# A decode attention kernel whose big loads move from SyncE's DMA queue to GpSimd's

## The chip, the core and the metric

The kernel runs on one core of a Trainium2 chip. A core has five engines with an instruction stream each: TensorE (PE; PEld is its weight load), VectorE (DVE), ScalarE (ACT), GpSimd (POOL) and SyncE (SP). They meet only through semaphores. Data comes from HBM into SBUF, an on-chip memory of 128 partitions, by DMA: an engine issues a transfer, 16 DMA engines carry it out, and a semaphore tells that it has landed. TensorE writes its results to PSUM, a second on-chip memory. The metric is the device time of one execution in microseconds; less is better.

## The reference

Eight sequences, one new token each, 32 heads of 128, and a cache of 4096 keys and values per head. All inputs are bf16.

```python
xn = layernorm(x)                                  # (8, 1, 640)
q = (xn @ wq) as (8, 32 heads, 1, 128)
p = softmax(q . k_cache / sqrt(128))               # k_cache, v_cache (8, 32, 4096, 128)
attn = (p . v_cache) joined over heads @ wo        # wo (4096, 640)
y = layernorm(xn)
mlp = gelu(y @ w1 + b1) @ w2 + b2                  # w1 (640, 1728), w2 (1728, 640)
out = x + attn + mlp
```

The two caches are 8 x 32 x 4096 x 128 x 2 bytes = 268.4 MB each. They are read once. With the weights this is nearly all that the kernel moves.

## The kernel before

The work is cut into 32 tiles (`NQ = 32`), each of 8 heads of one sequence. A tile of K, and a tile of V, is one load of 128 partitions x 64 KB = 8.39 MB: a partition holds 256 consecutive keys of one head. SBUF has three slots of this size in the tensor `S_sb`: K tiles alternate between slots KA and KB, all V tiles use the slot VS. The same slots hold the weights where no tile needs them: `wq` lies in VS at the start, the MLP weights in KA and the output weights `wo` in KB at the end.

What happens to a tile i:

- K(i) lands. POOL has waited for it and writes a flag, the memset of `kr_sb` (`k_ready`), which releases TensorE; VectorE waits for K(i) itself.
- For 80 of a partition's 256 keys, TensorE transposes K in groups of eight (`pe_T`, into `TR_ps`), ScalarE copies them to `KT_sb` (`act_T`), and TensorE multiplies with the query (`pe_QK`, into `S_ps`). The last of them gives the ticket `kt` or `qkl`.
- For the other 176 keys VectorE does it in three chunks (`dve_chunk`): multiply by the query in place (ticket `ym`), add one half to the other, reduce (the last chunk's ticket is `km`).
- VectorE finds the maximum (`dve_max`), ScalarE does the exponentials into `P_sb` (`act_exp`, ticket `exp`).
- When V(i) has landed, TensorE multiplies it with `P_sb` (`pe_PV`, 256 matmuls into `PV_ps`, ticket `pv`), ScalarE copies the result to `oU_sb`, and POOL scales it into `oT_sb` (`o_norm`).
- POOL also spreads the next tile's query over partitions (`qrep`, the copy to `qrep_sb`), once the last `pe_QK` of the tile before is done.

The order on each engine is written out by hand: `at(position, function, ...)` puts a step at a position on one axis, 100 per tile (`Q = 100.0`), and the steps are then called in that order, each adding its instructions to the lists of the engines it uses. An engine takes its own list strictly in order, and a wait holds all that stands behind it on that engine.

All big loads are on SyncE's list, K(i+1) ahead of V(i). K(i) waits until its slot is free: for i from 2 to 5 for `kt` and `km` of tile i-2, from `KLATE = 6` on for `exp` of tile i-2. V(i) waits for `pv` of tile i-1; V(0) and K(1) wait for `qmm`, the end of the query's matmuls. V(30), the last but one, is loaded in two pieces (`V_CUT`, 192 and 64 keys of each partition), so that `pe_PV` of tile 30 can start on the first; for this TensorE's loop has one more wait at key 192, on the semaphores `ld_vl`. The MLP weights (`load_mlp`) are issued after V(30), the output weights in six pieces (`load_wl`, `load_wn`) after V(31), which waits for `pv` of tile 30. Eight small loads (`load_w2b`) follow POOL's memset of their place. At the end the pieces of `wo` are multiplied in as they land, and the output is stored.

The profile knows nearly every instruction as line 111, the helper that writes it out (109 for waits); the tensor's names tell the steps apart.

Of the kernel before, what the change touches and what calls it, by code (L numbers as in the profile page):

```python
# [14 lines left out]
P = 128  # L15
# [177 lines left out]
def bass_parallel_sum__gqa_block_cached__mixer_channel_mlp__decode_kernel(  # L193
# [21 lines left out]
    NQ = NHQ * B  # L215
    DC = D // P
    FB = F // P
# [11 lines left out]
    NS = 2  # L229
    LOOP0, LOOPN = 2, 15  # L230
    KLATE = 6
    assert NKEY == 256 and NQ == 32
    SLOT = NKEY * DH
    KA, KB, VS = 0, 1, 2
# [1 line left out]
    RW = P // HW  # L236
    NL = 3
    WN_CUT = (0, 5 * CT, 7 * CT, 7 * CT + CT // 2, HS * CT)
    V_CUT = (0, 192, 256)

    def jp_of(i):
        return 80

    def chunks(i):
        jd = NKEY - jp_of(i)
        n = 3
        return [(jd * c // n, jd * (c + 1) // n) for c in range(n)]

    def kslot(i):
        return KA if i % 2 == 0 else KB  # L250
# [8 lines left out]
    with ExitStack() as es:  # L259
        sb = lambda name, shape, dt: es.enter_context(nc.sbuf_tensor(name, shape, dt))  # L260
        ps = lambda name, shape, dt: es.enter_context(nc.psum_tensor(name, shape, dt))
        sem = lambda name: es.enter_context(nc.semaphore(name))

        S_sb = sb("S_sb", [P, 3, SLOT], BF)
        tile = [S_sb[:, s, :].rearrange("p (j d) -> p j d", d=DH) for s in range(3)]
# [6 lines left out]
        def scratch(n, rows=P, slot=KB):  # L272
            ap = part(slot, o_[slot], n, rows)
            o_[slot] += n + n % 2
            return ap

        wq_sb = part(VS, 0, DC * H * DH).rearrange("p (c n) -> p c n", c=DC)
        w1_sb = scratch(DC * F, P, KA).rearrange("p (c n) -> p c n", c=DC)
        w2_sb = scratch(FB * D, P, KA).rearrange("p (c n) -> p c n", n=D)
# [20 lines left out]
        zeros_sb = scratch(P)  # L300
        assert max(o_.values()) <= SLOT

        ones_sb = sb("ones_sb", [1, B], BF)
# [16 lines left out]
        mx_sb = sb("mx_sb", [P, 32], F32)  # L320
        mxT_sb = sb("mxT_sb", [P, 32], F32)
        mq_sb = sb("mq_sb", [P, 2], F32)
        mb_sb = sb("mb_sb", [P, 32], F32)
# [20 lines left out]
        pe, dve, act, sp, pool = (_Eng(sem(f"{n}_s")) for n in ("pe", "dve", "act", "sp", "pool"))  # L344
        pe2, act2, fin, fin2 = (_Eng(sem(n)) for n in ("pe2_s", "act2_s", "fin_s", "fin2_s"))
        ld_s = [_Dma(sem(f"ld_s{s}")) for s in range(3)]
        ld_x, ld_b1, ld_b2, ld_wq, ld_w1, ld_w2a, ld_w2b, st_a, st_o = (
            _Dma(sem(n)) for n in ("ld_x", "ld_b1", "ld_b2", "ld_wq", "ld_w1", "ld_w2a", "ld_w2b", "st_a", "st_o"))
        ld_vl = [_Dma(sem(f"ld_vl{q}")) for q in range(1, len(V_CUT) - 1)]
        ld_wl = [_Dma(sem(f"ld_wl{q}")) for q in range(2)]  # L350
        ld_wn = [_Dma(sem(f"ld_wn{q}")) for q in range(len(WN_CUT) - 1)]
        tk = {}
        prog = []

        def at(pos, fn, *a):
            prog.append((pos, len(prog), fn, a))

        def load(key, dma, dst, src, eng=None):
            tk[key] = dma.sig((eng or sp).dma_start(dst, src))

        def cache_src(cache, i):
            hq, b = divmod(i, B)
            return cache[b, hq * HS:(hq + 1) * HS].rearrange("h (p j) d -> (h p) j d", j=NKEY)

        def load_k(i):
            s = kslot(i)
            if i >= KLATE:
                sp.wait(tk[("exp", i - 2)])
            elif i >= 2:
                sp.wait(tk[("kt", i - 2)], tk[("km", i - 2)])  # L370
            elif s == KB:
                sp.wait(tk["qmm"])
            tk[("k", i)] = ld_s[s].sig(sp.dma_start(tile[s], cache_src(A_k_cache, i)))

        def load_mlp():
            sp.wait(tk[("kt", NQ - 2)], tk[("km", NQ - 2)])
            load("w1", ld_w1, w1_sb, B_w1.rearrange("(p c) f -> p c f", c=DC))
            load("w2a", ld_w2a, w2_sb, B_w2[0:FB * P, :].rearrange("(p c) n -> p c n", c=FB))

        def load_v(i):  # L380
            sp.wait(tk["qmm"] if i == 0 else tk[("pv", i - 1)])
            if i != NQ - 2:
                tk[("v", i)] = [ld_s[VS].sig(sp.dma_start(tile[VS], cache_src(A_v_cache, i)))]
                return
            tk[("v", i)] = []
            for d, lo, hi in zip([ld_s[VS]] + ld_vl, V_CUT[:-1], V_CUT[1:]):
                if lo:
                    d.n += 1
                tk[("v", i)].append(
                    d.sig(sp.dma_start(tile[VS][:, lo:hi, :], cache_src(A_v_cache, i)[:, lo:hi, :])))  # L390

        def load_b1():
            act.wait(tk[("kt", NQ - 2)], tk[("km", NQ - 2)])
            load("b1", ld_b1, b1_sb, B_b1.rearrange("(o f) -> o f", o=1), act)

        def load_wl(q):
            sp.wait(tk[("kt", NQ - 1)], tk[("km", NQ - 1)])
            lo, hi = (0, HW) if q == 0 else (HW, HW + HS)
            tk[("wl", q)] = ld_wl[q].sig(sp.dma_start(
                woW_sb if q == 0 else woL_sb[:, 0, :],  # L400
                A_wo[lo * DH:hi * DH, :].rearrange("(p s) n -> p (s n)", p=P)))

        def load_wn(q):
            lo, hi = WN_CUT[q], WN_CUT[q + 1]
            n = HS * DH
            tk[("wn", q)] = ld_wn[q].sig(sp.dma_start(
                woL_sb[:, 1, lo * CN:hi * CN],
                A_wo[NL * n:(NL + 1) * n, :].rearrange("(p s) n -> p (s n)", p=P)[:, lo * CN:hi * CN]))

# [12 lines left out]
        def consts_pool():  # L422
            pool.iota(iota_h, [[-HP, HS]], base=0, channel_multiplier=1)
            pool.iota(iota_w, [[-RW, HW]], base=0, channel_multiplier=1)
            tk["iota"] = pool.sig(pool.iota(iota_i, [[1, P]], base=0, channel_multiplier=-1))
            for d, (ap, v) in zip([None] + ld_vl + [None] * 2, (
                    (zeros_sb, 0.0), (ones_sb[:, :], 1.0), (mx_sb[:, :], 0.0), (mb_sb[:, :], 0.0))):
                inst = pool.memset(ap, v)
                if d is not None:
                    inst.call[3] = (d.sem, 1)  # L430
            tk["consts"] = pool.sig(pool.memset(ones_f[:, :], 1.0))

        def sel_pool():
# [186 lines left out]
        def dve_chunk(i, c):  # L620
            s = i % 2
            lo, hi = chunks(i)[c]
            w = hi - lo
            kt = tile[kslot(i)][:, lo:hi, :]
            dve.wait(tk[("k", i)], tk[("qb", i)])
            t = dve.sig(dve.tensor_tensor(
                kt, kt, qbc_sb[:, s, :][:, None, :].to_broadcast([P, w, DH]), ALU.mult))
            tk[("ym", i)] = t
            dve.wait(t)
            t = dve.sig(dve.tensor_tensor(kt[:, :, 0:DH // 2], kt[:, :, 0:DH // 2], kt[:, :, DH // 2:DH], ALU.add))  # L630
            dve.wait(t, tk.get(("exp", i - 2)))
            tk[("km", i)] = dve.sig(dve.tensor_reduce(Sd_sb[:, s, lo:hi], kt[:, :, 0:DH // 2], AX.X, ALU.add))
# [56 lines left out]
        def pe_PV(i):  # L689
            PVB.use(pe)  # L690
            pe.wait(tk[("exp", i)])
            for j in range(NKEY):
                if j == 0:
                    pe.wait(tk[("v", i)][0])
                elif j in V_CUT:
                    pe.wait_ge(ld_vl[V_CUT.index(j) - 1].sem, 1)
                last = pe.matmul(PV_ps[:, 0:HS], tile[VS][:, j, :], P_sb[:, :, j],
# [110 lines left out]
        Q = 100.0  # L808
        at(-900, load, "x", ld_x, x_sb, x2, act)
        at(-898, load, "b2", ld_b2, b2_sb, B_b2.rearrange("(o f) -> o f", o=1), act)  # L810
        at(-890, load, "wq", ld_wq, wq_sb, A_wq.rearrange("(p c) n -> p c n", c=DC))
        at(NQ * Q - 55, load_mlp)
        at(NQ * Q - 54.9, load_w2b)
        at(-870, load_k, 0)
        at(NQ * Q - 60.1, zero_w2b)
        at(-800, consts_pool)
        at(-795, idents)
        at(NQ * Q - 60, sel_pool)
# [15 lines left out]
        for i in range(NQ):  # L834
            o = i * Q
            last = i == NQ - 1
            if i:
                at(o - 51, load_k, i)
            at(o + 50, load_v, i)
            at(o - 52, qrep, i)  # L840
            at(o - 2, k_ready, i)
            at(o - 11, pe_qbc, i)
            at(o - 10.5, act_qbc, i)
            nt = jp_of(i) // TPB
            w = 42.0 / nt
            for t in range(nt):
                at(o + w * t, pe_T, i, t)
                at(o + w * (t + 0.4), act_T, i, t)
                at(o + w * (t + 1.5), pe_QK, i, t)
            at(o + 2, dve_chunk, i, 0)  # L850
            at(o + 26, dve_chunk, i, 1)
            at(o + 52, dve_sel, i, 0)
            at(o + 55, dve_sel, i, 1)
            at(o + 58, dve_chunk, i, 2)
            at(o + 84, dve_max, i)
            at(o + 90 if i else o + Q + 45, act_exp, i)
            at(o + Q + 48, pe_RS, i)
            at(o + Q + 57, dve_rinv, i)
            at(o + Q + 50, pe_PV, i)
            if not last:  # L860
                at(o + Q + 71, act_O, i)
            at(o + Q + 75, o_norm, i)
# [3 lines left out]
        o = NQ * Q  # L866
        for q in range(2):
            at(o + 50 + 0.1 * q, load_wl, q)
            at(o + 79.1 + 0.2 * q, fin_wl, q)
# [74 lines left out]
```

## Time and profile before

| | |
|---|---|
| median of 3 runs | 1281.46 us (1281.36 to 1281.47) |
| profiled execution: span from first to last instruction | 1280.1 us; its time as a run isn't listed beside it |
| moved from HBM | 551.8 MB, 431 GB/s over the span |
| busy: DVE / PE / PEld / ACT / POOL | 86% / 52% / 45% / 37% / 9% |
| DMA queues | SP's carries 99.7%; POOL issues none |

A row of a timeline gives the start in microseconds from the span's start, the duration in microseconds, the engine, and the instruction as `out<-in`; brackets hold the idle time before it and what ended it. "SPq" is SyncE's instruction stream. Rows of the DMA issues give KB (where one size is in the group) and the microseconds from issue to landing. A row of windows begins with the window, then its length, the busy time of PE, PEld, DVE, ACT and POOL with counts, the granted TensorE clock, the DMA share and GB/s.

### The profile page before, as it was taken

How to read it: one execution, taken by the hardware profiler on the slowest of the kernel's cores; microseconds unless marked ns; L12 is line 12 of the kernel's file. 1: busy time of each engine (PE TensorE's matmuls, PEld its weight loads, DVE VectorE, ACT ScalarE, POOL GpSimd, SP SyncE). 2: the span in 40 equal slices, each digit the busy share in tenths (PEclk: the TensorE clock that was granted, in tenths of full speed). 3: DMA queues.
4: the chain of work that ended last, by engine and by line, in shares of the span. 5: the costliest groups of instructions: out<-in, count | busy, mean ns of one | idle time of the engine just before them, and what ended most of it. 6: DMA issues, size and time to landing. Idle time of an engine off the chain costs nothing.

```text
span 1280.1 us, 34355 instructions
## 1 busy us (share of the span) xinstructions
PE 672.0 (52%) x13906; PEld 573.2 (45%) x13906; DVE 1101.6 (86%) x681; ACT 477.0 (37%) x906; POOL 109.3 (9%) x119
## 2 busy tenths in 40 slices
PE   1636555446645446545456554456454466464476
PEld 1435444335535345444345444345343355353465
DVE  1899999889888889888898888898888898888894
ACT  0524444233444233443234443234442334442331
POOL 0020010000000000000000000000000000000050
PEclk9755565565565556555555555556555656655665
DMA  9999999999999999999999999999999999999998
GB/s 419 427 433 431 432 430 432 442 432 430 430 442 428 432 432 436 436 430 432 432 442 430 430 432 438 432 430 434 436 436 430 432 430 442 432 428 434 432 440 367
DMA packets 10785, 551.99 MB, mean 431 GB/s; under 512 B 1242, under 2 KB 1523, under 8 KB 1812
## 3 DMA queue, kind: packets, MB, share of 16 engines
q1 hardware_dynamic: 10736, 551.79, 99.7%
q8 instruction: 9, 0.15, 0.0%
q10 hardware_dynamic: 36, 0.02, 0.0%
q14 instruction: 4, 0.03, 0.0%
HBM read 551.80 MB, written 0.01 MB: 431 GB/s over the span
## 4 chain that ended last, share of the span: by engine, by line
DMA 47%; DVE 37%; issue 11%; ACT 4%; DVEq 0%; SPq 0%; PE 0%
DMA S_sb<-in_A_k_cache_dram 45%; DVE S_sb L111 26%; DVE Sd_sb L111 8%; ACT P_sb L111 4%; DMA S_sb<-in_A_wo_dram 2%; DVE S_ps L111 1%; DVE mx_sb L111 1%; DVE mbT_sb L111 0%; DVE mxT_sb L111 0%; DVE ri_sb L111 0%; DVE NB_sb L111 0%; DVEq L109 0%; DVE mq_sb L111 0%; DVE mb_sb L111 0%; SPq L111 0%
## 5 line engine op out<-in xcount | busy, mean ns | idle before, releaser
L111 PE MATMUL TR_ps<-ident_bf,S_sb 128*128 128x128 bf16 (+1 forms) x2570 | 343.3, 280 | 353.5 <-POOL kr_sb L111 333.2
L111 DVE TENSOR_TENSOR S_sb<-S_sb,qbc_sb 128x7552 bf16<-128x7552 bf16 (+1 forms) x96 | 388.7, 4049 | 128.3 <-DMA S_sb<-in_A_k_cache_dram 128.0
L111 PEld LDWEIGHTS TR_ps<-ident_bf,S_sb 128*128 (+2 forms) x2570 | 245.7, 103 | 411.7 <-issue 338.5
L111 DVE TENSOR_REDUCE Sd_sb<-S_sb 128x59 f32<-128x3776 bf16 (+1 forms) x96 | 390.2, 4065 | 6.0
L111 ACT ACTIVATE KT_sb<-TR_ps 128x1024 bf16<-128x1024 bf16 x320 | 327.0, 1024 | 121.6 <-PE TR_ps L111 109.6
L111 PE MATMUL PV_ps<-P_sb,S_sb 128*128 128x8 bf16 x8192 | 224.0, 175 | 140.6 <-DMA S_sb<-in_A_v_cache_dram 137.9
L111 PEld LDWEIGHTS PV_ps<-P_sb,S_sb 128*128 128x128 bf16 x8192 | 221.3, 103 | 143.3 <-DMA S_sb<-in_A_v_cache_dram 140.5
L111 DVE TENSOR_TENSOR S_sb<-S_sb 128x3776 bf16<-128x3776 bf16 (+1 forms) x96 | 206.5, 2151 | 3.3
L111 ACT ACTIVATE P_sb<-Sd_sb,NB_sb 128x256 bf16<-128x256 f32 x256 | 126.3, 494 | 210.9 <-DVE NB_sb L111 210.9
L111 PE MATMUL S_ps<-qrep_sb,KT_sb 128*128 128x8 bf16 x2560 | 121.9, 177 | 50.9 <-ACT KT_sb L111 47.8
L111 ACT ACTIVATE oU_sb<-PV_ps 128x8 f32<-128x8 f32 x31 | 5.5, 178 | 375.8 <-PE PV_ps L111 375.8
L111 PEld LDWEIGHTS S_ps<-qrep_sb,KT_sb 128*128 128x128 bf16 x2560 | 91.7, 103 | 82.4 <-ACT KT_sb L111 41.1
L111 POOL TENSOR_TENSOR oT_sb<-oU_sb,ri_sb 128x8 bf16<-128x8 f32 x31 | 71.8, 2315 | 370.8 <-DVE S_sb L111 315.3
L111 POOL COPY qrep_sb<-qT_sb 128x128 bf16<-128x128 bf16 x32 | 18.3, 573 | 474.7 <-PE S_ps L111 455.1
L111 ACT ACTIVATION_READ_ACCUMULATOR P_sb<-Sd_sb,NB_sb 128x1 f32 x256 | 47.8, 187 | 0.0
L111 DVE TENSOR_TENSOR S_ps<-S_ps,mask_sb 128x320 f32<-128x320 f32 (+1 forms) x65 | 31.6, 486 | 2.7 <-PE S_ps L111 2.7
L111 DVE TENSOR_REDUCE Sd_sb<-S_ps 128x40 f32<-128x320 f32 x64 | 31.5, 492 | 2.2
L111 PE MATMUL QB_ps<-ident_bf,qrep_sb 128*128 128x128 bf16 x32 | 9.1, 285 | 40.7 <-DVE S_sb L111 22.1
L111 ACT ACTIVATE qbc_sb<-QB_ps 128x128 bf16<-128x128 f32 x32 | 8.9, 278 | 57.6 <-PE QB_ps L111 57.6
L111 POOL MEMSET kr_sb<- 128x1 f32 x32 | 3.2, 99 | 294.9 <-DMA S_sb<-in_A_k_cache_dram 294.9
L111 PEld LDWEIGHTS QB_ps<-ident_bf,qrep_sb 128*128 128x128 bf16 x32 | 3.3, 103 | 43.6 <-ACT oU_sb L111 29.0
L111 PE MATMUL CH_ps<-rs_sb,ones_f 128*128 128x8 f32 x64 | 15.4, 313 | 6.5 <-ACT P_sb L111 6.5
(68 smaller groups left out, 150.6 us busy)
## 6 DMA issues: line engine op xcount, KB each, us to landing
S_sb<-in_A_v_cache_dram SPq DMA_DIRECT2D x1, 6144.0 KB, 26.8
S_sb<-in_A_wq_dram SPq DMA_DIRECT2D x1, 5120.0 KB, 15.6
S_sb<-in_A_wo_dram SPq DMA_DIRECT2D x1, 2560.0 KB, 18.4
S_sb<-in_B_w_dram SPq DMA_DIRECT2D x1, 2160.0 KB, 30.3
S_sb<-in_B_w_dram SPq DMA_DIRECT2D x1, 2080.0 KB, 34.9
S_sb<-in_A_v_cache_dram SPq DMA_DIRECT2D x1, 2048.0 KB, 31.4
S_sb<-in_A_wo_dram SPq DMA_DIRECT2D x1, 1280.0 KB, 21.1
S_sb<-in_A_wo_dram SPq DMA_DIRECT2D x1, 800.0 KB, 22.6
```

Source lines behind the costliest of these rows:

```text
L111: inst = getattr(e, name)(*a, **k)
```

## The change

From the third K and the first V on, the big loads are issued by POOL instead of SP, with semaphores of their own (`ld_g`); so are the MLP weights and the six pieces of `wo`. K(0), K(1), `wq`, the eight small loads and the store stay on SP. The loads that move are part of POOL's list now, at positions of their own: K(i) right after `k_ready` of tile i-1 (position `o - 101` instead of `o - 51`), the MLP weights ahead of `k_ready` of tile 31. V(0) waits in addition for `ym0`, VectorE's second multiply of tile 0. V(30) is loaded whole, and the wait inside `pe_PV` is gone. `PACKET` is empty and adds nothing.

```diff
-    V_CUT = (0, 192, 256)
+    V_CUT = (0, 256)
...
         def load_k(i):
             s = kslot(i)
+            if i < 2:
+                if s == KB:
+                    sp.wait(tk["qmm"])
+                tk[("k", i)] = ld_s[s].sig(sp.dma_start(tile[s], cache_src(A_k_cache, i)))
+                return
             if i >= KLATE:
-                sp.wait(tk[("exp", i - 2)])
-            elif i >= 2:
-                sp.wait(tk[("kt", i - 2)], tk[("km", i - 2)])
-            elif s == KB:
-                sp.wait(tk["qmm"])
-            tk[("k", i)] = ld_s[s].sig(sp.dma_start(tile[s], cache_src(A_k_cache, i)))
+                pool.wait(tk[("exp", i - 2)])
+            else:
+                pool.wait(tk[("kt", i - 2)], tk[("km", i - 2)])
+            tk[("k", i)] = ld_g[s].sig(pool.dma_start(tile[s], cache_src(A_k_cache, i), **PACKET))
...
         def load_v(i):
-            sp.wait(tk["qmm"] if i == 0 else tk[("pv", i - 1)])
-            if i != NQ - 2:
-                tk[("v", i)] = [ld_s[VS].sig(sp.dma_start(tile[VS], cache_src(A_v_cache, i)))]
-                return
-            tk[("v", i)] = []
-            for d, lo, hi in zip([ld_s[VS]] + ld_vl, V_CUT[:-1], V_CUT[1:]):
...
+            pool.wait(tk["qmm"], tk["ym0"]) if i == 0 else pool.wait(tk[("pv", i - 1)])
+            tk[("v", i)] = [ld_g[VS].sig(pool.dma_start(tile[VS], cache_src(A_v_cache, i), **PACKET))]
...
         def load_wl(q):
-            sp.wait(tk[("kt", NQ - 1)], tk[("km", NQ - 1)])
+            pool.wait(tk[("kt", NQ - 1)], tk[("km", NQ - 1)])
...
             tk[("ym", i)] = t
+            if i == 0 and c == 1:
+                tk["ym0"] = t
...
-        at(NQ * Q - 55, load_mlp)
+        at(NQ * Q - 102.5, load_mlp)
...
-                at(o - 51, load_k, i)
+                at(o - 51 if i < 2 else o - 101, load_k, i)
```

How POOL's list changes in a tile of the steady stretch; the copy to `qrep_sb` is the next tile's query, the operation on `oT_sb` scales the last tile's result, and the memset of `kr_sb` is the flag that K has landed:

```order
 L111 MEMSET kr_sb 128x1
+L111 DMA S_sb<-in_A_k_cache_dram 128x32768
 L111 COPY qrep_sb<-qT_sb 128x128
+L111 DMA S_sb<-in_A_v_cache_dram 128x32768
 L111 TENSOR_TENSOR oT_sb<-oU_sb,ri_sb 128x8
```

The next K is issued behind the flag of the present one, and V ahead of the scaling of the last result.

POOL's list around the last tiles; `in_B_w_dram` are the MLP weights, the copies from `ident_bf` build masks for the end, and the V load is that of tile 31:

```order
 L111 TENSOR_TENSOR oT_sb<-oU_sb,ri_sb 128x8
+L111 DMA S_sb<-in_B_w_dram 128x8640
+L111 DMA S_sb<-in_B_w_dram 128x8320
 L111 MEMSET kr_sb 128x1
 L111 MEMSET S_sb 48x1280
 L111 COPY S_sb<-ident_bf 128x2048
 L111 COPY S_sb<-ident_bf 128x1024
+L111 DMA S_sb<-in_A_v_cache_dram 128x32768
 L111 TENSOR_TENSOR oT_sb<-oU_sb,ri_sb 128x8
```

The MLP weights stand ahead of the last flag, and V(31) behind the copies for the masks.

SyncE's list at the same place; the two V loads with 24576 and 8192 elements a partition are the pieces of V(30):

```order
-L111 DMA S_sb<-in_A_v_cache_dram 128x24576
-L111 DMA S_sb<-in_A_v_cache_dram 128x8192
-L111 DMA S_sb<-in_B_w_dram 128x8640
-L111 DMA S_sb<-in_B_w_dram 128x8320
 L111 DMA S_sb<-in_B_w_dram 4x1280 x8
-L111 DMA S_sb<-in_A_v_cache_dram 128x32768
```

Only the eight small loads are left there, and nothing on SyncE waits for TensorE any more.

More of the change, by code (lines that the diff above doesn't have):

```diff
@@ L231, in bass_parallel_sum__gqa_block_cached__mixer_channel_mlp__decode_kernel @@
     KLATE = 6
+    PACKET = {}
     assert NKEY == 256 and NQ == 32
@@ L351, in bass_parallel_sum__gqa_block_cached__mixer_channel_mlp__decode_kernel @@
         ld_wn = [_Dma(sem(f"ld_wn{q}")) for q in range(len(WN_CUT) - 1)]
+        ld_g = [_Dma(sem(f"ld_g{s}")) for s in range(3)]
         tk = {}
@@ L366, in load_k @@
             s = kslot(i)
-            if i >= KLATE:
-                sp.wait(tk[("exp", i - 2)])
-            elif i >= 2:
-                sp.wait(tk[("kt", i - 2)], tk[("km", i - 2)])
-            elif s == KB:
-                sp.wait(tk["qmm"])
-            tk[("k", i)] = ld_s[s].sig(sp.dma_start(tile[s], cache_src(A_k_cache, i)))
+            if i < 2:
[3 more added lines that the diff above has]
+                return
+            if i >= KLATE:
+                pool.wait(tk[("exp", i - 2)])
+            else:
+                pool.wait(tk[("kt", i - 2)], tk[("km", i - 2)])
+            tk[("k", i)] = ld_g[s].sig(pool.dma_start(tile[s], cache_src(A_k_cache, i), **PACKET))
         def load_mlp():
-            sp.wait(tk[("kt", NQ - 2)], tk[("km", NQ - 2)])
-            load("w1", ld_w1, w1_sb, B_w1.rearrange("(p c) f -> p c f", c=DC))
-            load("w2a", ld_w2a, w2_sb, B_w2[0:FB * P, :].rearrange("(p c) n -> p c n", c=FB))
+            pool.wait(tk[("kt", NQ - 2)], tk[("km", NQ - 2)])
+            load("w1", ld_w1, w1_sb, B_w1.rearrange("(p c) f -> p c f", c=DC), pool)
+            load("w2a", ld_w2a, w2_sb, B_w2[0:FB * P, :].rearrange("(p c) n -> p c n", c=FB), pool)
         def load_v(i):
-            sp.wait(tk["qmm"] if i == 0 else tk[("pv", i - 1)])
-            if i != NQ - 2:
-                tk[("v", i)] = [ld_s[VS].sig(sp.dma_start(tile[VS], cache_src(A_v_cache, i)))]
-                return
-            tk[("v", i)] = []
-            for d, lo, hi in zip([ld_s[VS]] + ld_vl, V_CUT[:-1], V_CUT[1:]):
[L387 to L390, printed above, removed]
+            pool.wait(tk["qmm"], tk["ym0"]) if i == 0 else pool.wait(tk[("pv", i - 1)])
+            tk[("v", i)] = [ld_g[VS].sig(pool.dma_start(tile[VS], cache_src(A_v_cache, i), **PACKET))]
         def load_b1():
@@ L396, in load_wl @@
         def load_wl(q):
-            sp.wait(tk[("kt", NQ - 1)], tk[("km", NQ - 1)])
+            pool.wait(tk[("kt", NQ - 1)], tk[("km", NQ - 1)])
             lo, hi = (0, HW) if q == 0 else (HW, HW + HS)
-            tk[("wl", q)] = ld_wl[q].sig(sp.dma_start(
+            tk[("wl", q)] = ld_wl[q].sig(pool.dma_start(
                 woW_sb if q == 0 else woL_sb[:, 0, :],
@@ L405, in load_wn @@
             n = HS * DH
-            tk[("wn", q)] = ld_wn[q].sig(sp.dma_start(
+            tk[("wn", q)] = ld_wn[q].sig(pool.dma_start(
                 woL_sb[:, 1, lo * CN:hi * CN],
@@ L425, in consts_pool @@
             tk["iota"] = pool.sig(pool.iota(iota_i, [[1, P]], base=0, channel_multiplier=-1))
[L426 to L430, printed above, removed]
+            for ap, v in ((zeros_sb, 0.0), (ones_sb[:, :], 1.0), (mx_sb[:, :], 0.0), (mb_sb[:, :], 0.0)):
+                pool.memset(ap, v)
             tk["consts"] = pool.sig(pool.memset(ones_f[:, :], 1.0))
```

## The prediction, made before the result was known

> **What bounds the kernel.** I read the page's busy lines and DMA queues first, then the transfers of one stretch in the middle, then the rows of the engines that issue and consume there.
>
> ```profile
> span 1280.1 us, 34355 instructions
> DVE  1899999889888889888898888898888898888894
> DMA  9999999999999999999999999999999999999998
> q1 hardware_dynamic: 10736, 551.79, 99.7%
> ```
>
> One DMA queue, SyncE's (q1), moves 551.79 MB and keeps the 16 DMA engines busy 99.7% of the span. VectorE is busy too, but with breaks. In the middle two tiles of heads look like this, first the DMA of the stretch 500 to 577.4 us, then SyncE's issues and what released them:
>
> ```profile
> DMA packets 576, 33.55 MB, mean 434 GB/s; under 512 B 64, under 2 KB 64, under 8 KB 64
> q1 hardware_dynamic: 576, 33.55, 100.2%
> ...
> 1061.65 0.19 ACT L111 ACTIVATION_READ_ACCUMULATOR P_sb<-Sd_sb,NB_sb 128x1 f32 x1
> 1061.86 0.33 SPq L111 DMA_DIRECT2D S_sb<-in_A_k_cache_dram  x1
> 1061.96 0.10 POOL L111 MEMSET kr_sb<- 128x1 f32 x1 [9.87 <-DMA S_sb<-in_A_k_cache_dram]
> 1062.02 4.03 DVE L111 TENSOR_TENSOR S_sb<-S_sb,qbc_sb 128x7424 bf16<-128x7424 bf16 x1 [4.25 <-DMA S_sb<-in_A_k_cache_dram]
> 1081.30 7.00 PE L111 MATMUL PV_ps<-P_sb,S_sb 128*128 128x8 bf16 x256 [4.97 <-DMA S_sb<-in_A_v_cache_dram]
> 1088.33 0.33 SPq L111 DMA_DIRECT2D S_sb<-in_A_v_cache_dram  x1
> 1100.55 0.33 SPq L111 DMA_DIRECT2D S_sb<-in_A_k_cache_dram  x1
> ```
>
> 576 packets less 64 small semaphore ones are 512 = 4 loads x 128 rows: each row of 64 KB is one packet, and they fill the engines without a gap (100.2%). From K issue to K issue it is 1100.55 - 1061.86 = 38.69 us for one K and one V, so 19.35 us a load; VectorE waits 4.25 us and TensorE 4.97 us for data in each period. The stream is the bound, and two things can move the end: the rate at which rows pass, and any time in which the queue runs empty. How far ahead each load is issued is in the times from issue to landing (the first row K, the second V, minimum/median/maximum):
>
> ```profile
> DMA to landing us min/median/max: 25.5/38.7/38.8
> DMA to landing us min/median/max: 24.2/31.6/53.5
> S_sb<-in_A_wq_dram SPq DMA_DIRECT2D x1, 5120.0 KB, 15.6
> ```
>
> The load of wq finds an empty queue. 5120 KB (5.24 MB) at 434 GB/s are 12.1 us, so a load alone needs 15.6 - 12.1 = 3.5 us beside its bytes, and a K or V alone 3.5 + 19.35 = 22.85 us. What lands later than that was queued, and the difference is its margin: 15.85 us for the median K, 8.75 us for the median V, 1.35 us for the tightest V.
>
> **The change part by part.** *The steady stretch.* 30 K and 32 V loads, 62 x 8.39 = 520.1 MB, go to GpSimd's queue, with the two MLP weights and six pieces of wo; 62 + 2 + 6 = 70 DMAs. On SP each took 0.33 us of issue; that is saved and worth nothing, because SP only waits. On POOL they stand in line with its own three steps. K(i+1) now stands behind the memset on kr_sb, which waits for K(i): at 1061.96, 0.1 us after SP's issue, out of a margin of 15.85. Behind its wait for the exponentials stand the copy to qrep_sb, the V load and oT_sb; the exponentials ended at 1061.84, ahead of the memset, so nothing is held. V(i) waits for PV(i-1), whose end also releases the oT_sb behind it. Both are hidden by the margins above; if a POOL issue took over 8.75 us longer than SP's, V would start to leave gaps.
>
> *The price of a POOL issue.* The trace has no DMA issued by GpSimd. Call its delay beyond SP's E. It can be below nothing by SP's own 0.33 us at most. The nearest rows are POOL's copies over 128 partitions, one free, one beside a VectorE multiply:
>
> ```profile
> 120.99 0.29 POOL L111 COPY qrep_sb<-qT_sb 128x128 bf16<-128x128 bf16 x1 [24.37 <-PE S_ps L111]
> 70.11 4.17 POOL L111 COPY qrep_sb<-qT_sb 128x128 bf16<-128x128 bf16 x1 [14.51 <-PE S_ps L111]
> 70.10 4.02 DVE L111 TENSOR_TENSOR S_sb<-S_sb,qbc_sb 128x7424 bf16<-128x7424 bf16 x1
> 1216.82 1.16 POOL L111 MEMSET S_sb<- 48x1280 bf16 x1
> 1216.84 4.03 DVE L111 TENSOR_TENSOR S_sb<-S_sb,qbc_sb 128x7424 bf16<-128x7424 bf16 x1 [4.27 <-DMA S_sb<-in_A_k_cache_dram]
> 50.14 0.10 POOL L111 MEMSET oT_sb<- 128x8 bf16 x1
> 50.09 2.12 DVE L111 TENSOR_TENSOR S_sb<-S_sb 128x3776 bf16<-128x3776 bf16 x1
> ```
>
> The copy reads SBUF and is held until the multiply ends (4.17 against 0.29 us: 3.9 us more). The two memsets only write, and end in 1.16 and 0.10 us while VectorE multiplies and adds. An issue reads no tile; it writes a list of 128 reads and 128 writes. I take twice the free copy, E = 0.6 us, with the ends -0.3 and 3.9. In the Trainium skill, SBUF — State Buffer, the box on the "DVE blocks DMA" trap under "SBUF: two separate sides" says that GpSimd cannot write descriptors while VectorE holds the shared port; its part "Who interferes with whom" takes tensor_tensor out of that, since it holds the read side only. By the first E would be 3.9, by the second under 1; the memset rows agree with the second, and no row here shows an issue.
>
> *The start.* V(0) was issued at 21.25 and waits now also for the second multiply of tile 0, and stands behind a copy. K(2) and V(2) have the least ahead of them:
>
> ```profile
> 21.25 0.43 SPq L111 DMA_DIRECT2D S_sb<-in_A_v_cache_dram  x1
> 68.64 0.33 SPq L111 DMA_DIRECT2D S_sb<-in_A_k_cache_dram  x1
> 128.20 0.33 SPq L111 DMA_DIRECT2D S_sb<-in_A_v_cache_dram  x1
> 48.83 1.37 POOL L111 COPY qrep_sb<-qT_sb 128x128 bf16<-128x128 bf16 x1 [12.86 <-PE S_ps L111]
> ```
>
> V(0) landed at 21.25 + 53.5 = 74.75. Issued at 48.83 + 1.37 = 50.2, alone it lands at 73.05: margin 1.7 us. K(2): 25.5 - 22.85 = 2.65 us. V(2): 24.2 - 22.85 = 1.35 us. K(1) stays on SP and shares the engines with V(0) at the end; bytes and end are the same, and VectorE wants K(1) only at 70.1. With E = 0.6 nothing is lost; beyond E = 1.35 the tightest, V(2), loses E - 1.35, and the others lie inside that loss.
>
> *The tail.* Tile 30's V came in two pieces, so that PV(30) could start on the first; V(31) waits for PV(30).
>
> ```profile
> 1204.45 0.80 SPq L111 DMA_DIRECT2D S_sb<-in_A_v_cache_dram  x2
> S_sb<-in_A_v_cache_dram SPq DMA_DIRECT2D x1, 2048.0 KB, 31.4
> 1231.32 6.98 PE L111 MATMUL PV_ps<-P_sb,S_sb 128*128 128x8 bf16 x256 [0.38 <-DMA S_sb<-in_A_v_cache_dram]
> 1238.33 0.34 SPq L111 DMA_DIRECT2D S_sb<-in_A_v_cache_dram  x1
> S_sb<-in_A_v_cache_dram SPq DMA_DIRECT2D x1, 27.2
> ```
>
> The second piece was issued near 1204.85 and landed 31.4 us later, at 1236.25, where the whole V(30) would. PV(30) then runs 1236.3 to 1243.3, 5 us later than before, and V(31) is issued at 1243.3 + E. Before, it landed at 1238.33 + 27.2 = 1265.53, behind the MLP weights; now alone it lands at 1243.3 + 22.85 + E = 1266.15 + E, 0.62 + E later. This is the one place where the queue runs out. The 5.24 MB of wo queue behind V(31) and the last matmuls wait for them, so that shift is the end's: 1.2 us with E = 0.6, 0.3 with -0.3, 4.5 with 3.9. POOL itself is free there: its two copies for sel_sb end at 1228.5, as in this row:
>
> ```profile
> 1217.92 10.54 POOL L111 COPY S_sb<-ident_bf 128x2048 bf16<-128x2048 bf16 x2
> ```
>
> The MLP weights are asked for by POOL after the same condition as before, ahead of kr_sb of tile 31, and have 30 us in the queue; the wo pieces follow 12 us before V(31) has landed. The eight small w2b loads stay on SP. One wait and a split run of matmuls leave TensorE's loop: nothing, since TensorE waits 4.97 us a tile.
>
> *The rate.* 520.1 MB at 434 GB/s are 1198.4 us, so 0.2% of rate is 2.4 us. The row size and count stay, and rows pass without gaps now; I take the same rate. Bounds are the fastest and the two slowest full-load stretches of this trace (the last columns are DMA share and GB/s):
>
> ```profile
> 94.20:113.50 19.30, 6.57 (x75) 5.02 (x75) 18.80 (x12) 8.31 (x22) 2.41 (x2) 0.50 1.01 436
> 35.80:55.40 19.60, 11.26 (x161) 9.43 (x161) 19.42 (x6) 11.69 (x13) 1.52 (x3) 0.81 0.99 429
> 15.50:35.80 20.30, 4.71 (x161) 4.45 (x161) 0.42 (x1) 0.28 (x1) 0.29 (x1) 1.00 0.97 417
> ```
>
> *Sum.* The profiled execution spans 1280.1 us; the runs' median is 1281.46, so 1.4 us lie around the span, which I carry over. 1280.1 + 1.2 = 1281.3 in the profile, 1282.7 us as a run.
>
> **The rivals.** *A faster stream.* If rows issued by GpSimd pass at 436 GB/s, 520.1 MB take 1192.9 us, 5.5 less: 1277.2 us. For it: the rate is all that bounds. Against it: rows are already back to back. The Trainium skill's DMA: Bandwidth & Descriptors, under "Anatomy of one DMA — SWDGE (gpsimd) path", fits GpSimd's DMAs with 2.0 us plus bytes over 436 GB/s, which is this case; its table under "Bandwidth" has 425 GB/s at 16 MB, which is the next but one. Neither is shown here.
>
> *Issues held by VectorE* (slower). At every load POOL meets a multiply or an add of VectorE; if writing the list is held like the copy at 70.11, E = 3.9: V(2) loses 3.9 - 1.35 = 2.55 and V(31) 4.5, together 7.1: 1288.5 us. In the middle 3.9 stays under 8.75. It decides from E = 1.65 on, where (E - 1.35) + (E + 0.62) passes 2.56 us. Against it are the memsets.
>
> *A slower stream.* If GpSimd's lists are fetched or cut otherwise, rows may pass at 429 GB/s: 1212.4 us, 14 more, with the tail 1296.7 us; at 417 it is 1247.2 and 1331. Nothing in the trace speaks for it but that no such queue is seen here. By the skill's 425 it would be 1223.8 us for the loads, some 25 us more in all, an estimate from that page.
>
> **How the numbers follow.** 0.2% of 1281.46 is 2.56 us, about what can be told from no change. Same rate with a small E (0.3 to 1.6): chance 0.42, time 1282.7, own range 1281.5 to 1284. Faster stream 0.22. Held issues 0.15. Slower stream 0.18. Something else in POOL's order, such as a wait that holds K for over 15 us: 0.03, slower. So faster 0.22, same 0.42, slower 0.36. The range for 8 in 10 reaches from 1276, below the faster stream, over the held issues to 1294, which leaves out the greater part of the slower stream and its far end: 0.42 + 0.18 + 0.14 + 0.07 is 0.81.
>
> **What would show it.** A new DMA queue with about 530 MB at 434 GB/s, still one packet per 64 KB row, and 38.7 us from kr_sb to kr_sb: the rate is right; 38.5 or 39.1 would show the rivals. V(31) landing about 1.2 us later with TensorE's last wait for V longer by that: the tail is right. Gaps in the DMA near 75, 133 and 1247 us, with POOL's issues ending when VectorE's add ends, would show held issues. Gaps in the middle would make the whole argument wrong.

## The result and the profile after

The changed kernel takes 1283.36 us (median of 20 runs, 1282.47 to 1284.16), the kernel before 1281.45 (20 runs beside it, 1281.16 to 1282.34). The ratio is 1.0014, with a 95% interval of 1.0008 to 1.0020: 1.9 us slower at the medians, inside the 0.2% that the prediction calls no change, but no longer nothing. The profiled execution of the changed kernel spans 1281.6 us and took 1282.87, against a span of 1280.1 before: 1.5 us more. It is this 1.5 us that the traces can place.

From the page of the changed kernel: the span, the DMA slices, the DMA queues (packets, MB, share), and further down the V loads with the median time from issue to landing:

```profile
span 1281.6 us, 34317 instructions
...
DMA  9999999999999999999999999999999999999998
...
q0 software_dynamic: 9824, 529.68, 95.6%
q1 hardware_dynamic: 512, 22.11, 4.0%
...
S_sb<-in_A_v_cache_dram POOLq DMA_DIRECT2D x32, 31.4
```

GpSimd's queue q0 carries what was moved, and q1 what stayed: 22.11 MB are K(0), K(1), wq and the small ones. The 16 engines are as full as before. The DMA of the same stretch in the middle as before, 500 to 577.4 us:

```profile
DMA packets 576, 33.55 MB, mean 434 GB/s; under 512 B 64, under 2 KB 64, under 8 KB 64
...
q0 software_dynamic: 576, 33.55, 100.2%
```

Same number of packets, same bytes, same 434 GB/s, same 100.2%: to the stream it makes no difference here which engine asks. The timeline of the changed kernel, first the start, then an issue of V under a multiply, one period in the middle, and the tail:

```profile
48.05 2.23 POOL L111 COPY qrep_sb<-qT_sb 128x128 bf16<-128x128 bf16 x1 [12.00 <-PE S_ps L111]
50.44 0.70 POOL L111 DMA_DIRECT2D S_sb<-in_A_v_cache_dram  x1 [0.16 <-issue]
57.80 0.10 POOL L111 MEMSET kr_sb<- 128x1 f32 x1 [6.54 <-DMA S_sb<-in_A_k_cache_dram]
...
127.05 4.04 DVE L111 TENSOR_TENSOR S_sb<-S_sb,qbc_sb 128x7552 bf16<-128x7552 bf16 x1
128.54 0.53 POOL L111 DMA_DIRECT2D S_sb<-in_A_v_cache_dram  x1 [7.20 <-PE PV_ps L111]
133.94 0.10 POOL L111 MEMSET kr_sb<- 128x1 f32 x1 [2.76 <-DMA S_sb<-in_A_k_cache_dram]
...
1062.80 0.10 POOL L111 MEMSET kr_sb<- 128x1 f32 x1 [9.87 <-DMA S_sb<-in_A_k_cache_dram]
1062.86 4.03 DVE L111 TENSOR_TENSOR S_sb<-S_sb,qbc_sb 128x7424 bf16<-128x7424 bf16 x1 [4.25 <-DMA S_sb<-in_A_k_cache_dram]
1063.04 0.57 POOL L111 DMA_DIRECT2D S_sb<-in_A_k_cache_dram  x1
1101.49 0.10 POOL L111 MEMSET kr_sb<- 128x1 f32 x1 [9.87 <-DMA S_sb<-in_A_k_cache_dram]
...
1217.62 0.10 POOL L111 MEMSET kr_sb<- 128x1 f32 x1 [4.44 <-DMA S_sb<-in_A_k_cache_dram]
1237.27 7.00 PE L111 MATMUL PV_ps<-P_sb,S_sb 128*128 128x8 bf16 x256 [5.28 <-DMA S_sb<-in_A_v_cache_dram]
1244.57 0.53 POOL L111 DMA_DIRECT2D S_sb<-in_A_v_cache_dram  x1 [15.27 <-PE PV_ps L111]
1267.10 5.08 PE L111 MATMUL PV_ps<-P_sb,S_sb 128*128 128x8 bf16 x184 [6.33 <-DMA S_sb<-in_A_v_cache_dram]
```

From flag to flag it is 1101.49 - 1062.80 = 38.69 us, as before. An issue takes POOL 0.53 or 0.57 us, SP's took 0.33. Both rows lie under a multiply of VectorE, 1063.04 inside 1062.86 to 1066.89 and 128.54 inside 127.05 to 131.09, and both issues end long before it, so no multiply holds them. The 0.57 goes with the K loads, the 0.53 with V.

Where the 1.5 us went can be read from the flags on `kr_sb`, one for each K that has landed. The same flags of the kernel before, those of K(1), K(3) and K(31), and its last run of matmuls:

```profile
55.50 0.10 POOL L111 MEMSET kr_sb<- 128x1 f32 x1 [5.25 <-DMA S_sb<-in_A_k_cache_dram]
...
133.09 0.10 POOL L111 MEMSET kr_sb<- 128x1 f32 x1 [1.97 <-DMA S_sb<-in_A_k_cache_dram]
...
1216.78 0.10 POOL L111 MEMSET kr_sb<- 128x1 f32 x1 [9.89 <-DMA S_sb<-in_A_k_cache_dram]
...
1265.62 6.54 PE L111 MATMUL PV_ps<-P_sb,S_sb 128*128 128x8 bf16 x239 [5.92 <-DMA S_sb<-in_A_v_cache_dram]
```

| | before | after | later by |
|---|---|---|---|
| K(1) has landed | 55.50 | 57.80 | 2.30 |
| K(3) has landed | 133.09 | 133.94 | 0.85 |
| K(31) has landed | 1216.78 | 1217.62 | 0.84 |
| last matmuls with V start | 1265.62 | 1267.10 | 1.48 |

0.85 us are lost before K(3), nothing in the 28 tiles up to K(31), and another 1.48 - 0.84 = 0.64 after it. The end follows the last matmuls with V by 14.5 us in both (1280.1 - 1265.62 and 1281.6 - 1267.10). So the loss has two places, the start and the tail, and the issues by the slower engine in between cost nothing.

### The profile page after: what moved, and what is told of

Its sections match the earlier page's. It is cut to its first block, busy times and chain, and to the rows that moved or that the text cites. A ratio compares the mean times of both kernels' runs of the same rounds, so it can differ in the third digit from the quotient of the medians.

```text
span 1281.6 us, 34317 instructions
## 1 busy us (share of the span) xinstructions
PE 672.3 (52%) x13906; PEld 574.8 (45%) x13906; DVE 1101.8 (86%) x681; ACT 476.3 (37%) x906; POOL 127.2 (10%) x189
## 3 DMA queue, kind: packets, MB, share of 16 engines
q1 hardware_dynamic: 512, 22.11, 4.0%
## 4 chain that ended last, share of the span: by engine, by line
DMA 82%; DVE 13%; issue 3%; ACT 0%; POOL 0%; PE 0%; DVEq 0%; SPq 0%
DMA S_sb<-in_A_k_cache_dram 81%; DVE S_sb L111 9%; DVE Sd_sb L111 3%; DMA S_sb<-in_A_wo_dram 2%; DVE S_ps L111 0%; ACT P_sb L111 0%; DVE mx_sb L111 0%; POOL kr_sb L111 0%; PE ACC_ps L111 0%; DVE mxT_sb L111 0%; DVE mbT_sb L111 0%; POOL S_sb L111 0%; DVE mq_sb L111 0%; DVE ri_sb L111 0%; DVE mb_sb L111 0%
## 5 line engine op out<-in xcount | busy, mean ns | idle before, releaser
L111 POOL TENSOR_TENSOR oT_sb<-oU_sb,ri_sb 128x8 bf16<-128x8 f32 x31 | 53.9, 1738 | 7.3 <-DVE ri_sb L111 6.9
L111 POOL DMA_DIRECT2D S_sb<-in_A_v_cache_dram x32 | 17.1, 533 | 365.2 <-DVE S_sb L111 315.5
L111 PEld LDWEIGHTS QB_ps<-ident_bf,qrep_sb 128*128 128x128 bf16 x32 | 3.3, 103 | 44.0 <-ACT oU_sb L111 26.9
## 6 DMA issues: line engine op xcount, KB each, us to landing
S_sb<-in_A_wo_dram POOLq DMA_DIRECT2D x1, 800.0 KB, 22.5
S_sb<-in_A_v_cache_dram POOLq DMA_DIRECT2D x32, 31.4
```

The lines of the kernel that those rows point to most:

```text
L111: inst = getattr(e, name)(*a, **k)
```

## The experiments

The theory: a late issue costs only where no other load stands before it in the queue. Its rivals: a price on each load from GpSimd's queue, or on each late issue, or a cost of the change of queue itself. Times below are medians with their extremes; the ratio is to the kernel before on the same chip (1281.49 and 1281.44 and, for the last two kernels, 1281.59). The flags' delays are against the first profile of before.

### V(30) in two pieces again

```diff
-    V_CUT = (0, 256)
+    V_CUT = (0, 192, 256)
```

Both pieces are issued by POOL; that the second has landed is told to TensorE by a one-column memset of POOL's.

> The changed kernel with V(30) in two pieces again, both issued by POOL; TensorE learns of the second through a POOL memset that waits for it. Late loads (the stream runs at the old rate, and the 1.9 us lost are V(0) and V(31) asked for too late): V(31) is issued 5 us earlier, its landing no longer shifts by 0.7 us, so about 0.7 us of the 1.9 come back: 1282.7 us. Cost of the source (a load from GpSimd costs something by itself, at the change of queue or at each load, wherever it is issued): nothing comes back, 1283.4 us.

1282.76 us (1282.27 to 1284.49), ratio 1.0012 (1.0003 to 1.0021), span 1281.0. V(31) was issued at 1239.42 and landed 26.9 us later, so it was queued again. From the flag of K(31), at 1217.31, to the last matmuls it took 1266.42 - 1217.31 = 49.11 us, against 48.84 before and 49.48 in the changed kernel. So the cut gives back some of the tail, in the direction of the theory, but 0.27 us stays, and the medians (1282.76 and 1283.36) are closer than their scatter.

### All big loads in one queue

`wq`, K(0), K(1) and V(0) also go to POOL, in SP's old order and with SP's old waits.

```diff
-                    sp.wait(tk["qmm"])
+                    pool.wait(tk["qmm"])
...
-            pool.wait(tk["qmm"], tk["ym0"]) if i == 0 else pool.wait(tk[("pv", i - 1)])
+            pool.wait(tk["qmm"] if i == 0 else tk[("pv", i - 1)])
...
-            at(o + 50, load_v, i)
+            at(o + 50 if i else -59, load_v, i)
```

> The changed kernel with wq, K(0), K(1) and V(0) on POOL as well, in the order and with the waits that SyncE had, so that one queue carries the stream from the start and V(0) is asked for at 21 us instead of 50. Late loads: the 0.85 us lost where V(0) follows K(1) come back; wq may start some tenths later: 1282.5 to 1282.9 us. Cost of the source by the change of queue: the same gain. Cost of the source at each load: 1283.4 us or more.

1283.02 us (1282.64 to 1285.38), ratio 1.0016 (1.0007 to 1.0025), span 1281.2: between the 1282.5 to 1282.9 of late loads and the 1283.4 of a cost at each load. The start of its timeline:

```profile
1.27 0.69 POOL L111 DMA_DIRECT2D S_sb<-in_A_wq_dram  x1 [0.82 <-POOLq L923]
...
1.96 0.54 POOL L111 DMA_DIRECT2D S_sb<-in_A_k_cache_dram  x1
...
36.72 0.10 POOL L111 MEMSET kr_sb<- 128x1 f32 x1 [13.54 <-DMA S_sb<-in_A_k_cache_dram]
56.38 0.10 POOL L111 MEMSET kr_sb<- 128x1 f32 x1 [5.29 <-DMA S_sb<-in_A_k_cache_dram]
```

K(1) is no longer delayed against K(0): 56.38 - 36.72 = 19.66 us, a load's own time, where the changed kernel has 57.80 - 35.95 = 21.85 (its flag of K(0) comes at 35.95). So the loss at the join of the two queues is gone. But a new one of the same size has come: the first flag is at 36.72 instead of 35.87, because POOL asks for `wq` at 1.27 us and for K(0) at 1.96, where SP did at 0.74 and 1.20. All flags stay 0.8 us late to the end. The tail from the flag of K(31) is 49.12 us.

### Both together

> Both edits together: one queue from the start and V(30) in two pieces. Late loads: 1281.8 us, the kernel before within 0.4 us. Cost of the source at each load: 1283.4 us.

1282.95 us (1282.53 to 1284.81), ratio 1.0012 (1.0003 to 1.0021), span 1281.5; the flags are 0.9 us late at K(0) and 1.1 to 1.2 from K(3) on, the tail is 49.18 us. The 1281.8 us that late loads would give did not come: a kernel with all big loads in GpSimd's queue and nothing late in its order was not as fast as the kernel before. Of the 1.4 us in its span 0.9 are there at K(0), whose load starts later.

### Only the cut of V(30), in the kernel before

```diff
-    V_CUT = (0, 192, 256)
+    V_CUT = (0, 256)
```

> The kernel before, all loads on SyncE, with V(30) loaded whole: the one part of the change that has nothing to do with the queue. Late loads: V(31) is issued 5 us later, at 1243.3, and lands 0.62 us later: 1282.1 us. If the 2.9 us for which the MLP weights still keep the queue busy at that moment hide it: 1281.45 us.

1281.53 us (1281.27 to 1282.26), ratio 1.0001 (0.9992 to 1.0010), span 1280.5. The timeline, with the issue of V(31) by SP and the matmuls that wait for it:

```profile
1236.14 7.00 PE L111 MATMUL PV_ps<-P_sb,S_sb 128*128 128x8 bf16 x256 [4.88 <-DMA S_sb<-in_A_v_cache_dram]
1243.17 0.34 SPq L111 DMA_DIRECT2D S_sb<-in_A_v_cache_dram  x1
...
1265.97 6.20 PE L111 MATMUL PV_ps<-P_sb,S_sb 128*128 128x8 bf16 x226 [1.45 <-DMA S_sb<-in_A_v_cache_dram]
```

The DMA issues of the same stretch, the landing of V(31) in the last column, here and then in the changed kernel:

```profile
S_sb<-in_A_v_cache_dram SPq DMA_DIRECT2D x1, 22.8
```

```profile
S_sb<-in_A_v_cache_dram POOLq DMA_DIRECT2D x1, 22.5
```

V(31) is now alone in the queue and lands 22.8 us after its issue. From the flag of K(31), at 1216.81, to the last matmuls it is 49.16 us, 0.32 more than before: the cut alone is worth a third of a microsecond, about half of the tail's loss, and nothing that the medians show. In the changed kernel POOL issued V(31) 0.30 us after the end of the matmuls (1244.57 against 1237.27 + 7.00), SP here 0.03 us after, but POOL's landed after 22.5 us instead of 22.8. So the price of a POOL issue, against an SP issue in an empty queue, is about nothing.

### V(0) asked for early, by SP

```diff
-            pool.wait(tk["qmm"], tk["ym0"]) if i == 0 else pool.wait(tk[("pv", i - 1)])
+            if i == 0:
+                sp.wait(tk["qmm"])
+                tk["v0"] = ld_s[VS].sig(sp.dma_start(tile[VS][:, 0:255, :], cache_src(A_v_cache, 0)[:, 0:255, :]))
+                pool.wait(tk["qmm"], tk["ym0"])
+                tk[("v", 0)] = [ld_g[VS].sig(pool.dma_start(tile[VS][:, 255:256, :], cache_src(A_v_cache, 0)[:, 255:256, :]))]
+                return
+            pool.wait(tk[("pv", i - 1)])
```

255 of the 256 keys of each partition come through SP's queue behind K(1) as before, the last key where the changed kernel has the whole load. TensorE waits for both.

> The changed kernel with V(0) asked for by SyncE at 21 us as in the kernel before; only the last of its 256 keys of each partition is left to POOL, at the old moment, so that the semaphores count as before. Late loads: the flag of K(31) comes about 1180.9 us after that of K(0) as in the kernel before, not 1181.7, and 0.5 to 0.8 us come back: about 1282.7 us. Cost of the change of queue: V(0) and K(2) change it instead of K(1) and V(0), so 1283.4 us. Cost of the source at each load: 1283.4 us.

The start is mended. In its timeline, SP's issue of V(0), POOL's issues of the rest and of K(2), and the flags of K(1) and K(3); then V(0) among its DMA issues:

```profile
20.76 0.43 SPq L111 DMA_DIRECT2D S_sb<-in_A_v_cache_dram  x1
...
50.42 0.70 POOL L111 DMA_DIRECT2D S_sb<-in_A_v_cache_dram  x1 [0.16 <-issue]
55.63 0.10 POOL L111 MEMSET kr_sb<- 128x1 f32 x1 [4.39 <-DMA S_sb<-in_A_k_cache_dram]
...
68.91 0.54 POOL L111 DMA_DIRECT2D S_sb<-in_A_k_cache_dram  x1 [13.18 <-DVE Sd_sb L111]
...
133.11 0.10 POOL L111 MEMSET kr_sb<- 128x1 f32 x1 [1.95 <-DMA S_sb<-in_A_k_cache_dram]
```

```profile
S_sb<-in_A_v_cache_dram SPq DMA_DIRECT2D x1, 8160.0 KB, 56.5
```

K(3) is 0.02 us late, not 0.85. So the 0.85 us hang on the 8 MB of V(0) coming late through the other queue, not on the POOL issue at 50.4 us, which is still there. The place where the queues join has moved to V(0) and K(2), which POOL asks for at 68.91, some 6 us before V(0) landed in the kernel before (74.75): V(0) lands at 20.76 + 56.5 = 77.26 us, 2.5 later, as K(1) is 2.3 late in the changed kernel, and nothing is lost. Not every join costs, then. The run as a whole gained little: 1283.10 us (1281.68 to 1283.67), ratio 1.0010 (1.0001 to 1.0019), the profiled span 1281.8. From the flag of K(0) to that of K(31) it is 1181.76 us, not the 1180.9 that late loads would give, for in this profile the flags slip again, by 0.24 us at K(9) and by 0.66 at K(30), where the changed kernel's don't. In both places the DMA view has a packet of another queue; here 325 to 340 us:

```profile
q14 instruction: 1, 0.01, 0.1%
```

A fetch of instructions shares an engine with the rows of V and K and could push it behind the others. But the changed kernel has such a packet in the same two stretches and no slip there, so the place alone does not show a cause; it was not tested. The eleven runs fall into two groups, 1281.68 to 1282.15 and 1282.84 to 1283.67, so a loss of about 1 us came and went between executions of one kernel.

### V(0) asked for at 40 us, in the other queue

```diff
-            if i == 0 and c == 1:
+            if i == 0 and c == 0:
...
-            at(o + 50, load_v, i)
+            at(o + 50 if i else o + 30, load_v, i)
```

> The changed kernel with V(0) asked for by POOL some 10 us earlier, after VectorE's first multiply of tile 0 and ahead of the copy to qrep_sb; both queues then share the engines for longer, and K(1) lands later, near 68 us. Late loads: the loss where V(0) follows K(1) goes, 0.5 to 0.8 us come back: about 1282.7 us. Cost of the change of queue: 1283.4 us or more, since the shared time is longer.

1288.82 us (1288.52 to 1290.12), ratio 1.0058 (1.0044 to 1.0072): the first expectation missed, and of the second only "or more" held, by way of V(1) as the rows show. The start of its timeline and the next issue of V:

```profile
40.49 0.71 POOL L111 DMA_DIRECT2D S_sb<-in_A_v_cache_dram  x1 [4.55 <-PE TR_ps L111]
67.28 0.10 POOL L111 MEMSET kr_sb<- 128x1 f32 x1 [17.06 <-DMA S_sb<-in_A_k_cache_dram]
...
97.15 0.53 POOL L111 DMA_DIRECT2D S_sb<-in_A_v_cache_dram  x1 [12.72 <-PE PV_ps L111]
```

Two queues share the engines. K(1) had some 11 us to its landing when V(0)'s rows began (44.9 us), and lands 67.28 - 55.50 = 11.8 us later. The Trainium skill's DMA: Bandwidth & Descriptors, under "SWDGE vs HWDGE vs iDMA", says that each DMA engine goes round robin between its queues; this row agrees, with half the rate for each. All of tile 1 then waits, V(1) is asked for only at 97.15, and the queue runs dry. The window 90 to 100 us (last columns: clock, DMA share, GB/s):

```profile
90.00:100.00 10.00, 3.04 (x109) 2.87 (x105) 9.86 (x9) 0.18 (x1) 1.58 (x3) 0.50 0.44 161
```

At a share of 0.44, some 5.6 of the 10 us are lost; the flags are 6.8 us late at K(3) and 6.9 at K(31). Nothing of it is made up. So the late place of V(0) in the changed kernel is no oversight: ten microseconds earlier in the other queue is much worse, because K(1) then no longer comes first.

### V(0) late, but in SP's queue

The kernel before, with the wait of the changed one.

```diff
-            sp.wait(tk["qmm"] if i == 0 else tk[("pv", i - 1)])
+            sp.wait(tk["ym0"] if i == 0 else tk[("pv", i - 1)])
```

> The kernel before, all on SyncE, with V(0) waiting for VectorE's second multiply of tile 0, so that it is asked for at 50 us. Late loads: about the same loss as in the changed kernel, 0.3 to 0.8 us: 1281.8 to 1282.3 us. Cost of the change of queue: there is none, 1281.5 us.

1281.65 us (1281.28 to 1282.55), ratio 1.0002 (0.9993 to 1.0011), span 1280.2.

```profile
50.09 0.33 SPq L111 DMA_DIRECT2D S_sb<-in_A_v_cache_dram  x1
55.33 0.10 POOL L111 MEMSET kr_sb<- 128x1 f32 x1 [5.07 <-DMA S_sb<-in_A_k_cache_dram]
```

Issued at 50.09 us, 0.35 earlier than by POOL, V(0) costs nothing in SP's queue: K(1) is not late, and all later flags are within 0.2 us of before. The loss of 0.3 to 0.8 us that late loads would bring did not come, so a late issue alone isn't it. What differs is seen in the DMA packets that start from 53.0 to 53.5 us, when the engines end K(1), first in the kernel before, then in the changed one:

```profile
DMA packets 20, 0.66 MB, mean 1311 GB/s; under 512 B 10, under 2 KB 10, under 8 KB 10
```

```profile
DMA packets 15, 0.33 MB, mean 655 GB/s; under 512 B 10, under 2 KB 10, under 8 KB 10
```

The ten small packets are the semaphore packets with which ten engines end K(1). Before, ten rows of V(0) start in that time; in the changed kernel only five, the first at 53.3 us, 2.9 after the issue. Some engines have nothing to carry for a moment: the stream runs dry before K(1) has landed. At the join of V(0) and K(2) in the kernel above, 72 to 74.5 us, it doesn't:

```profile
q0 software_dynamic: 16, 1.05, 97.7%
q1 hardware_dynamic: 3, 0.13, 12.1%
```

There 16 rows of K(2) start while just one semaphore packet of V(0) has gone. That a load lands 2.3 or 2.5 us late at a join is thus no loss by itself: its last semaphore packet (at 57.4 us for K(1)) stands behind one row of the other queue, and a row of 64 KB takes an engine 2.42 us. Not separated is whether V(0)'s rows come too late because of the other queue, or because POOL's issue comes 0.35 us later and takes 0.70 instead of 0.33 us.

### V(0) by SP, and V(30) in two pieces

> The changed kernel with V(0) on SyncE and V(30) in two pieces. Late loads: what is left are the two tenths by which a POOL issue is later, about 1281.9 us. Cost of the source: 1282.8 us, as with V(30) in two pieces alone.

1282.51 us (1281.82 to 1283.67), ratio 1.0009 (1.0000 to 1.0018), span 1280.7. The median lies between the two expectations. The start is mended, the tail only in part: the flag of K(31) is 0.17 us late and the tail 49.25 us, 0.41 over before. The profiled span is 0.6 us over before's, the median 1.07 over. Against the changed kernel's 1.9 us the two edits give back not quite half, but the intervals of the two ratios overlap, and the runs don't settle what makes the rest.

### Every V issue held for 6 and for 12 us

What hides a late issue in the middle was reckoned from landing times only. Here it is measured: chained memsets between the end of the matmuls of V(i-1) and the issue of V(i), in the tiles 8 to 27; ten as shown in the first kernel, twenty in the second.

```diff
             pool.wait(tk["qmm"], tk["ym0"]) if i == 0 else pool.wait(tk[("pv", i - 1)])
+            if 8 <= i <= 27:
+                for _ in range(10):               
+                    pool.wait(dly.sig(pool.memset(dly_sb[:, :], 0.0)))
```

> The changed kernel, with ten small memsets in a chain on GpSimd (each waits for the one before) between the wait for the matmuls of V(i-1) and the issue of V(i), for the 20 tiles 8 to 27. Nothing is left out of the computation. The chain's length d is read from the trace; from the memsets seen so far about 0.5 to 0.8 us each, so d is 5 to 8 us. If the margin of 8.75 us of the median V is real, the issues come d later, V lands as before (the DMA share stays at 100%, 38.7 us from flag to flag) and the time is that of the changed kernel, 1282.5 to 1284.2 us. If a late issue costs wherever it is, as at the start, the time is up to 20 x d = 100 to 160 us more.

> The same with twenty memsets, so d is 10 to 16 us. By the margin each of the 20 tiles grows by d - 8.75 us: 1283.4 + 20 x (d - 8.75), which is 1308 to 1428 us for d of 10 to 16; a period of 38.7 + d - 8.75 between flags, and gaps in the DMA in each of these tiles. If the margin is larger than reckoned from the landing times, the period stays at 38.7 us and the time at 1283.4. If each late issue costs in full, the time grows by 20 x d = 200 to 320 us.

With ten, 1283.35 us (1282.87 to 1284.30), ratio 1.0015 (1.0004 to 1.0027), the time of the changed kernel. One tile in its timeline, and from its page the median time from issue to landing of V in the whole run:

```profile
579.36 7.00 PE L111 MATMUL PV_ps<-P_sb,S_sb 128*128 128x8 bf16 x256 [5.17 <-DMA S_sb<-in_A_v_cache_dram]
586.42 5.76 POOL L111 MEMSET dly_sb<- 128x512 bf16 x10 [11.89 <-PE PV_ps L111]
592.48 0.53 POOL L111 DMA_DIRECT2D S_sb<-in_A_v_cache_dram  x1 [0.30 <-POOL dly_sb L111]
```

```profile
S_sb<-in_A_v_cache_dram POOLq DMA_DIRECT2D x32, 25.5
```

The issue comes 592.48 - 586.36 = 6.12 us after the matmuls, 5.8 later than without the memsets, and V lands 25.5 us after its issue instead of 31.4: 5.9 us of queueing are used up, and nothing is lost.

With twenty, 1332.45 us (1331.20 to 1333.70, two runs), ratio 1.0396 (1.0366 to 1.0426). Its timeline over one tile, and the landing of V in the DMA issues of 500 to 582 us:

```profile
553.01 7.00 PE L111 MATMUL PV_ps<-P_sb,S_sb 128*128 128x8 bf16 x256 [3.08 <-DMA S_sb<-in_A_v_cache_dram]
560.07 11.59 POOL L111 MEMSET dly_sb<- 128x512 bf16 x20 [10.20 <-PE PV_ps L111]
571.96 0.53 POOL L111 DMA_DIRECT2D S_sb<-in_A_v_cache_dram  x1 [0.30 <-POOL dly_sb L111]
594.13 7.00 PE L111 MATMUL PV_ps<-P_sb,S_sb 128*128 128x8 bf16 x256 [3.26 <-DMA S_sb<-in_A_v_cache_dram]
```

```profile
S_sb<-in_A_v_cache_dram POOLq DMA_DIRECT2D x2, 22.1
```

The issue is 11.65 us later than without. The period is 594.13 - 553.01 = 41.12 us, which is 7.0 of matmuls, 11.95 to the issue and 22.1 to the landing: now that chain is the bound, not the stream. It is 2.4 us over 38.7, and 20 times that, 49 us, is the whole difference to the changed kernel. The margin is therefore 11.65 - 2.4 = 9.2 us, not 8.75, since a V alone lands in 22.1 to 22.5 us and not in 22.85. A price on each late issue is excluded by the first kernel, and a cover without an end by the second.

## Why the prediction was right or wrong

The time, 1283.36 us, lies 0.7 us over the 1282.7 predicted, inside the range of 1281.5 to 1284 that the likeliest case was given, and 0.14% slower is what was called no change. By its steps:

- **The stream bounds, at the same rate.** Right: 434 GB/s in the same stretch, 38.69 us from flag to flag. Both rivals about the rate fell, the faster (436) and the slower (429) stream. Of the figures in the Trainium skill's DMA: Bandwidth & Descriptors neither the 436 GB/s of the fit nor the 425 of the table showed; the fit's 2.0 us beside the bytes were 22.1 to 22.5 less 19.35, some 2.8 to 3.2.
- **The steady stretch is covered.** Right, and the margin of V is measured at 9.2 us where the sum had 8.75. The moved issues add nothing between K(3) and K(31).
- **The price E of an issue.** Taken at 0.6 us, between -0.3 and 3.9. In the empty queue of the tail it is 0.27 us of later issue less 0.3 us of sooner landing, about nothing. The choice of the memsets' rows over the copy's row was right: issues aren't held by VectorE's multiplies. The rival of held issues fell. The Trainium skill's SBUF — State Buffer, under "Who interferes with whom", agrees, by inference: tensor_tensor takes only the read side of the shared port. The box on the "DVE blocks DMA" trap speaks of VectorE's two-port modes, which that part says tensor_tensor does not have, so the box was no ground for E = 3.9 here.
- **The start.** Wrong. The step that failed is V(0)'s margin of 1.7 us, with which nothing was to be lost. It asked only when V(0) is wanted, and held that "bytes and end are the same" while K(1) shares the engines with it. The runs show 0.85 us lost there for good (0.5 us with V(30) in two pieces, 1.2 us in the run with the short hold), gone when V(0) goes through SP, early or late, or when all loads are in POOL's queue. The first row of V(0) came 2.9 us after the issue, and by then the first engines had ended K(1). In a kernel that the stream bounds the question at each load is not whether it lands in time for its user, but whether the engines pass from one load to the next without a break.
- **The tail.** Right in mechanism, mis-sized. The sum had 0.62 + E = 1.2 us; the profile has 0.64. The 0.62 for V(30) in one piece measured 0.32 in SP's queue, because a load alone lands in 22.8 us or less and TensorE was done a little sooner than reckoned. With all loads in POOL's queue and V(30) whole the tail is 49.12 us, against 49.16 in SP's, so there the queue adds nothing. The other 0.32 us of the changed kernel are lost before V(31) is asked for: from the flag of K(31) to the matmuls with V(30) it takes 1237.27 - 1217.62 = 19.65 us, in SP's queue 1236.14 - 1216.81 = 19.33. Why V(30) comes later there, and why 0.27 to 0.41 us stay with V(30) in two pieces, isn't settled.
- **The sum.** 1.2 us against 1.5 in the profiled spans: 0.85 at the start that was put at nothing, and 0.64 at the tail that was put at 1.2. The near hit is partly two errors against each other. The medians differ by 0.4 us more; this is within the scatter of the changed kernel.

No kernel tried beats the kernel before. Two equal it, and both load through SP: V(30) whole, and V(0) late.

## What to carry to other kernels

When a DMA stream is the bound, read each issue's margin as its landing time less that of a load alone; a later issue or a slower issuing engine is free up to there and costs in full beyond, and what was lost here was never made up. Look first at the ends of the stream and at places where it passes from one queue to another: within a queue a load stands behind the last one in order, while two queues share the engines. There the margin runs to the moment when the first engine has nothing left to carry, not to the moment when the data is wanted or the load before has landed. Before moving loads to another engine, look at when that engine can issue its first.

## What was not expected of the hardware

- V(0), issued by POOL 5 us before K(1) would land, cost 0.5 to 1.2 us, since its first row started 2.9 us after the issue and some engines had run dry; issued by SP 0.35 us sooner, or at a join with 6 us to go, nothing was lost.
- At a join the earlier load lands a row of the other queue later (2.3 and 2.5 us, a row takes 2.42), whether time is lost or not.
- The first DMA of the kernel is asked for by POOL at 1.27 us and takes 0.69, by SP at 0.74 and 0.40 us; K(0) landed 0.85 us later for it.
- A load alone lands no later when POOL issues it (22.1 to 22.5 us for 8.39 MB) than when SP does (22.8), though the issue itself takes 0.53 us instead of 0.33.
- Kernels that load through GpSimd scatter more from run to run: eleven runs of one kernel lie within 1.85 to 2.74 us, eleven of the two that load through SP within 0.99 and 1.27. The cause stays open.
